# One accumulator of the first batch's first transform moves to another set of PSUM banks

## The chip, the cores and the metric

The kernel runs on one core of one Trainium2 chip. The metric is the device time of one execution in microseconds (us). Four compute engines matter: TensorE (PE, with PEld for its weight loads), VectorE (DVE), ScalarE (ACT) and GpSimd (POOL); SP only issues DMAs. TensorE writes its results into PSUM, eight banks of 2 KB per partition, from which DVE and ACT take them.

## The reference

Four batches, each of 768 positions and 8 heads of 48 channels, go through three layers: a linear recurrence (here done in chunks of 96), a token mixer that takes the real part of a 2-D Fourier transform, and two dense blocks.

```python
attn_out = _attn_ref(**attn_kwargs)              # per head: S = a*S + k v^T (a complex), y = q . Re(S)
x = attn_out.transpose(0, 2, 1, 3).reshape(B, S, H * D)   # 4 x 768 x 384
# _moe_ref
X = np.fft.fft(x, axis=1)
X = np.fft.fft(X, axis=2)
u = x + np.real(X)
un = (u - mean(u)) / np.sqrt(var(u) + 1e-06)
x = u + np.maximum(un @ w_ch1, 0.0) @ w_ch2
# _moe2_ref: a token mixer (w_tok1, w_tok2) and a second dense block (w_ch1, w_ch2), both added to x
```

## The kernel before

Each batch has a chain and a dense part. The chain is the scan and the attention chunks (`stage1`), then the Fourier mixer with its normalisation (`stage2`), then the transposes of the normalised rows (`transposed`). The dense part (`mlp`, `tok1`, `tok2`, `mlp2`) is nearly all matmuls of 128x128 weights with 384 columns (lines L1034, L1056, L1260, L1278). The dense part of one batch runs beside the chain of the next. The chain of the first batch has no dense work beside it: TensorE's long run starts when that chain ends. To keep TensorE occupied there, `warm` (L347) puts in matmuls whose results nobody reads. The weights arrive as 64-bit floats. `convert` turns each half block into a pair of fp32r blocks in six steps on ACT (L214, L219, L239), DVE (L227, L233) and POOL (L229, L240), loads it on SP (L206) and stores the result for the later batches (L244). Twelve half blocks whose loads came early are converted beside the first batch's `stage2`; most of the others follow, one by one, beside the first batch's dense part.

A planner in the compiler's tile layer puts the instructions in order before the run. Each instruction has a priority (class `Prio`: by stream, then by place in the program), and the planner places the ready one of the best priority on each engine, by its own estimate of times, and gives each new tile a free bank of its tag. On the chip each engine then works strictly in that order.

PSUM tiles come from `palloc(tag, shape)`. The tags have 8 banks in all: `s` 2, `l` 3, `p` 2, `c` 1. A call with `"s"` is spread over several tags by a counter, `turn3`, that goes up by one at each such call: while `lent` is 0, as in the whole chain of the first batch, the tags are s, s, c in turn; later it is s alone (scan of batch 1) or s and p in turn (its `stage2`), then s, s, c again. A call with `"l"` leaves the counter alone. In `stage2` of the first batch, `l` serves `warm` and the small tiles `q` of the normalisation; afterwards it serves the dense part.

In `stage2`, `folds` (L1093, L1099) and `mirrors` (L1109, and copies of single columns, L1116) prepare four kinds of rows, `ty` 0 to 3. `dft(1)` and then `dft(0)` run the first transform: for each `ty` four fp32 matmuls, which are eight instructions in the trace (L1125), into one PSUM tile, and one ACT copy of it into `Z` (L1127). With the counter as it stands, `dft(1)` gets the tags s, c, s, s and `dft(0)` gets c, s, s, c for `ty` 0 to 3; the program as built runs the four of `dft(0)` in the order 1, 2, 0, 3. Then come three rounds `i`: the second transform (`smm`, L1152, L1157), an ACT copy of its result (L1188), its difference and sum on POOL (L1189, L1190), transposes of the tokens (L1199), four additions into `u` on DVE (L1204), the statistics, a Newton step for the inverse root (L1221 to L1226) and the normalised rows (L1231 on ACT, L1233 on DVE). Round 0 reads `Z` of `ty` 0 and 1, round 1 all four, round 2 `ty` 2 and 3.

Of the kernel before, what the change touches and what calls it, by code (L numbers as in the profile page):

```python
# [54 lines left out]
def attn_fft_mixer_kernel(ctx: ExitStack, tc: tile.TileContext, aL, xL, vL, wL, qN, kN, vN, arN, aiN,  # L55
# [47 lines left out]
    def palloc(tag, shape):  # L103
        n = 1
        for s in shape[1:]:
            n *= s
        if tag == "s":
            turn3[0] += 1
            tag = ("ssc", "s", "sp")[lent[0]]
            tag = tag[turn3[0] % len(tag)]  # L110
        t = psum.tile([128, 512], F32, tag=tag, bufs=PSB[tag], name=tag)
        v = t[0:shape[0], 0:n]
        if len(shape) == 3:
            v = v.rearrange("p (a b) -> p a b", b=shape[2])
        return v
# [952 lines left out]
    def stage2(b, space):  # L1068
# [50 lines left out]
        def dft(kt):  # L1119
            for ty in range(4):  # L1120
                n0, n = 128 * kt, ZK[ty][kt]
                ps = palloc("s", [128, 2, 97])
                for r in range(2):
                    for dt in range(2):
                        te.matmul(out=ps[0:n, r, :], lhsT=fd[:, ty, r, dt, n0:n0 + n], rhs=dcos[0:112, ty % 2, dt, r, :],  # L1125
                                  start=(dt == 0), stop=(dt == 1))
                se.copy(out=Z[0:n, 2 * ty + kt, :].rearrange("p (i r) -> p r i", r=2), in_=ps[0:n])  # L1127

        for k, (o, n) in enumerate(XP[b][:-1]):
            folds(k, o, n)  # L1130
        mirrors(*NR[0])
        dft(1)
        folds(len(XP[b]) - 1, *XP[b][-1])
        x = mirrors(*NR[1])
        if b == 0:
# [4 lines left out]
            for _ in range(5):  # L1140
                tick(0)
            rests[0] = None
        dft(0)

        if b == 0 and WZ:
# [29 lines left out]
        for i in range(3):  # L1175
            ps = palloc("s", [128, 2, 193])
# [285 lines left out]
```

## Time and profile before

| | |
|---|---|
| median of 3 runs | 1025.44 us (1022.24 to 1027.12) |
| profiled execution | 1025.11 us |
| its span (first to last instruction) | 1023.2 us |
| PE busy | 951.0 us, 93% of the span |
| DVE, ACT, POOL busy | 716.9, 526.4, 452.8 us |

The busy time is summed over the whole span, and the share of the first batch's chain differs much from that of the rest. The profile is of one execution; what lies outside its span is 1.9 us.

### The profile page before, as it was taken

To read this page: it belongs to the slowest core of one execution; us is meant where nothing else is said; L and a number is where in the kernel's file an instruction comes from. 1 tells how busy PE (TensorE), PEld (TensorE's weight loads), DVE (VectorE), ACT (ScalarE), POOL (GpSimd) and SP (SyncE) were. 2 spreads that over 40 slices of the span, in tenths; PEclk is the share of its full clock that TensorE was granted. 3 is DMA by queue.
4 is the path that set the end of the run, shared out by engine and by line. 5 is a ranking of instruction groups with operands and counts; after the bars stand their busy time and mean duration, and the time that the engine had idled before them with its cause. 6 is when DMAs were issued, how large, how long until landed. Compare 5 with 4: busy or idle time off the path is not lost.

```text
span 1023.2 us, 21015 instructions
## 1 busy us (share of the span) xinstructions
PE 951.0 (93%) x7312; PEld 902.0 (88%) x7312; DVE 716.9 (70%) x1965; ACT 526.4 (51%) x1489; POOL 452.8 (44%) x655
## 2 busy tenths in 40 slices
PE   1479989999899999999999999999999999999997
PEld 0338869999898899999998999999989999999997
DVE  7988978889897778999668889855664333433332
ACT  7864568887995166887216667821342122211111
POOL 7744677765785673677147335614630002000000
PEclk9999999999999999999999999999999999999999
DMA  6625865886689435665734467553325345435422
GB/s 234 175 67 140 290 269 165 283 268 210 212 258 272 146 95 187 193 179 174 206 110 140 129 193 247 157 149 102 108 78 166 131 131 171 139 108 176 136 91 80
DMA packets 98337, 173.09 MB, mean 169 GB/s; under 512 B 10928, under 2 KB 57904, under 8 KB 97712
## 3 DMA queue, kind: packets, MB, share of 16 engines
q1 hardware_dynamic: 98224, 171.67, 53.8%
q8 instruction: 60, 0.98, 0.4%
q14 instruction: 53, 0.43, 0.1%
HBM read 132.31 MB, written 39.32 MB: 168 GB/s over the span
## 4 chain that ended last, share of the span: by engine, by line
PE 66%; DVE 6%; ACT 3%; DMA 2%; POOL 2%; issue 2%; SPq 0%; POOLq 0%; ACTq 0%; DVEq 0%
PE l L1056 25%; PE l L1034 23%; DMA cvt<-wL 2%; PE s L845 2%; PE s L721 2%; PE l L1260 1%; PE l L1278 1%; PE s L1260 1%; PE s L1278 1%; PE s L1152 1%; DVE qkt L1099 1%; PE s L900 1%; PE s L860 1%; PE c L721 1%; PE c L845 1%
## 5 line engine op out<-in xcount | busy, mean ns | idle before, releaser
L1056 PE MATMUL l<-w,h 128*128 128x384 f32 x1728 | 324.0, 339 | 1.5 <-DVE h L1047 1.0
L1034 PE MATMUL l<-th,w 128*128 128x384 f32 x1152 | 313.3, 341 | 2.8 <-DVE h L1047 2.5
L1056 PEld LDWEIGHTS l<-w,h 128*128 128x128 f32 x1728 | 298.2, 188 | 3.5 <-DVE h L1047 2.0
L1034 PEld LDWEIGHTS l<-th,w 128*128 128x128 f32 x1152 | 209.1, 188 | 5.8 <-DVE h L1047 3.9
L1038 ACT ACTIVATE h<-l 128x384 fp32r<-128x384 f32 x192 | 94.0, 490 | 215.9 <-PE l L1034 215.3
L1034 PE MATMUL l<-tl,w 128*128 128x384 f32 x576 | 194.6, 338 | 0.0
L1059 DVE TENSOR_TENSOR u<-u,l 128x384 f32<-128x384 f32 x192 | 105.5, 549 | 74.4 <-PE l L1056 73.4
L1047 DVE SCALAR_TENSOR_TENSOR h<-l,h 128x384 fp32r<-128x384 f32 x160 | 88.3, 552 | 88.9 <-ACT h L1038 88.8
L1034 PEld LDWEIGHTS l<-tl,w 128*128 128x128 f32 x576 | 108.4, 188 | 0.1
L229 POOL TENSOR_TENSOR cvt<-cvt 128x384 int32<-128x384 int32 x48 | 50.4, 1051 | 27.4 <-DVE cvt L225 16.5
L1245 POOL TENSOR_TENSOR xl<-u,xh 128x384 fp32r<-128x384 f32 x18 | 18.0, 1014 | 93.2 <-ACT xh L1244 93.0
L240 POOL TENSOR_TENSOR w<-cvt,w 128x384 fp32r<-128x384 f32 x44 | 45.0, 1027 | 13.1 <-ACT w L239 13.0
L1045 POOL TENSOR_TENSOR h<-full,h 128x384 fp32r<-128x384 f32 x32 | 32.5, 1016 | 34.3 <-ACT full L1044 32.8
L529 PE MATMUL s<-misc,y 128*112 128x128 f32 x64 | 14.5, 369 | 35.4 <-DVE y L511 27.9
L694 DVE TENSOR_TENSOR p<-p,A 128x144 f32<-128x144 f32 x144 | 44.7, 310 | 2.8 <-ACT A L671 1.0
L529 PEld LDWEIGHTS s<-misc,y 128*112 128x112 f32 x64 | 9.3, 177 | 41.6 <-POOL ss L496 20.3
L881 POOL TENSOR_TENSOR yc<-Aa,gm 48x384 f32<-48x384 f32 x18 | 20.6, 1147 | 53.3 <-DVE Aa L871 53.0
L670 POOL TENSOR_TENSOR A<-raw,tm 128x144 f32<-128x144 f32 (+1 forms) x51 | 25.9, 508 | 39.4 <-DVE yt L695 29.6
L696 DVE TENSOR_TENSOR p<-p,yt 128x96 f32<-128x96 f32 x144 | 37.7, 262 | 2.8
L651 POOL TENSOR_TENSOR tm<-tm 128x144 f32<-128x144 f32 (+1 forms) x51 | 25.3, 496 | 32.3 <-ACT tm L650 27.8
L695 DVE TENSOR_TENSOR yt<-p,A 128x96 f32<-128x96 f32 x144 | 36.2, 251 | 2.4 <-ACT A L674 0.5
L721 PE MATMUL s<-misc,y 128*112 128x128 f32 x222 | 35.5, 273 | 1.2 <-DVE y L708 0.8
(320 smaller groups left out, 2045.2 us busy)
## 6 DMA issues: line engine op xcount, KB each, us to landing
w<-wscr SPq DMA_DIRECT2D x180, 384.0 KB, 3.5
cvt<-wL SPq DMA_DIRECT2D x48, 384.0 KB, 4.8
wscr<-w SPq DMA_DIRECT2D x44, 384.0 KB, 4.1
Kn<-kn SPq DMA_DIRECT2D x56, 192.0 KB, 3.7
kn<-y SPq DMA_DIRECT2D x96, 96.0 KB, 2.7
raw<-aL SPq DMA_DIRECT2D x48, 144.0 KB, 3.8
xx<-xL SPq DMA_DIRECT2D x48, 144.0 KB, 3.6
V<-vL SPq DMA_DIRECT2D x32, 144.0 KB, 3.0
```

The costliest lines, as they stand in the source:

```text
L229: x = ge.tensor_tensor(out=a, in0=a, in1=lo, op=ALU.add)
L240: ge.tensor_tensor(out=parts[:, 1, :], in0=a.bitcast(F32), in1=r32(parts[:, 0, :]), op=ALU.subtract)
L694: ve.tensor_tensor(out=cur, in0=prev, in1=A[:, j, 0:3, :], op=ALU.mult)
L695: ve.tensor_tensor(out=y, in0=prev[:, 1::-1, :], in1=A[:, j, 3:5, :], op=ALU.mult)
L696: ve.tensor_tensor(out=cur[:, 0:2, :], in0=cur[:, 0:2, :], in1=y, op=ALU.add)
L721: te.transpose(ps[:, j, :], y[:, j, 0:112], ident)
L1034: te.matmul(out=ps, lhsT=w1[:, wi, kt * 128:kt * 128 + 128], rhs=x[g][:, kt, :], start=(n == 0), stop=(n == 8))
L1038: x = se.activation(out=hi, in_=ps, func=ACTF.Relu)
L1045: ge.tensor_tensor(out=lo, in0=full, in1=r32(hi), op=ALU.subtract)
L1047: ve.scalar_tensor_tensor(out=lo, in0=ps, scalar=0.0, in1=r32(hi), op0=ALU.max, op1=ALU.subtract)
L1056: te.matmul(out=ps, lhsT=hs[m][:, hi, tt * 128:tt * 128 + 128], rhs=w2[:, wi, :], start=(n == 0), stop=(n == 8))
L1059: ve.tensor_tensor(out=u[tt], in0=u[tt], in1=ps, op=ALU.add)
```

## The change

One call of `palloc` in `dft` takes the tag `l` where it took `s`, for the first batch, the second call (`kt` = 0) and the fourth kind (`ty` = 3). The counter `turn3` therefore stands one lower at every later call with `"s"`, in this and all later batches: where the order was s, c, s, s | c, s, s, c | s, s, c, ... it is s, c, s, s | c, s, s, l | c, s, s, ...

```diff
@@ -1119,7 +1119,7 @@
         def dft(kt):
             for ty in range(4):
                 n0, n = 128 * kt, ZK[ty][kt]
-                ps = palloc("s", [128, 2, 97])
+                ps = palloc("l" if b == 0 and not kt and ty == 3 else "s", [128, 2, 97])
                 for r in range(2):
                     for dt in range(2):
```

## Rows read from the trace of the kernel before

**Rows 1.** The page: span, then busy time of each engine.
```profile
span 1023.2 us, 21015 instructions
...
PE 951.0 (93%) x7312; PEld 902.0 (88%) x7312; DVE 716.9 (70%) x1965; ACT 526.4 (51%) x1489; POOL 452.8 (44%) x655
```
**Rows 2.** Windows by stage: stretch, length, busy us per engine, granted clock, DMA.
```profile
0.00:155.00 155.00, 103.77 (x951) 79.10 (x952) 128.92 (x399) 98.32 (x273) 97.11 (x143) 0.96 0.62 194
155.00:1023.00 868.00, 847.27 (x6362) 822.90 (x6360) 588.01 (x1567) 428.06 (x1217) 355.71 (x513) 1.00 0.53 165
...
155.00:360.00 205.00, 195.05 (x1566) 185.28 (x1564) 174.69 (x461) 152.49 (x432) 143.93 (x191) 1.00 0.71 226
```
**Rows 3.** Timeline of PE: start, duration, line, out<-in, count, idle before and releaser.
```profile
126.73 1.03 PE L1125 MATMUL s<-dcos,qkt 112*128 112x97 f32 x8
...
128.59 1.02 PE L1125 MATMUL s<-dcos,qkt 112*128 112x97 f32 x8
129.45 1.06 PE L1125 MATMUL c<-dcos,qkt 112*128 112x97 f32 x8
131.71 1.13 PE L1125 MATMUL c<-dcos,qkt 112*128 112x97 f32 x8 [1.20 <-ACT qkt L1127]
132.68 1.50 PE L1152 MATMUL s<-qkt 128*128 128x193 f32 x8
...
155.15 1.34 PE L1034 MATMUL l<-th,w 128*128 128x384 f32 x3
```
**Rows 4.** Timeline of ACT, 131 to 141 us.
```profile
131.33 0.33 ACT L1127 COPY qkt<-c 128x194 f32<-128x194 f32 x1
132.58 0.52 ACT L214 ACTIVATE p<-cvt 128x384 f32<-128x384 f32 x1 [0.93 <-DVE cvt L233]
...
133.44 0.34 ACT L1127 COPY qkt<-c 128x194 f32<-128x194 f32 x1
134.22 0.48 ACT L1188 COPY qkt<-s 128x386 f32<-128x386 f32 x1 [0.45 <-PE s L1152]
...
140.89 0.48 ACT L1188 COPY qkt<-s 128x386 f32<-128x386 f32 x1
```
**Rows 5.** Timeline of POOL, 134 to 144 us, and a window of its run.
```profile
134.80 1.02 POOL L229 TENSOR_TENSOR cvt<-cvt 128x384 int32<-128x384 int32 x1
135.77 0.54 POOL L1189 TENSOR_TENSOR qkt<-qkt 128x193 f32<-128x193 f32 x1
...
143.53 0.53 POOL L1189 TENSOR_TENSOR qkt<-qkt 128x193 f32<-128x193 f32 x1
...
129.98:145.49 15.51, 13.74 (x80) 10.85 (x80) 12.18 (x30) 8.69 (x25) 15.51 (x19) 1.00 0.72 286
```
**Rows 6.** Timeline of DVE, 136 to 149 us.
```profile
136.34 0.85 DVE L1204 TENSOR_TENSOR u<-s,qkt 128x192 f32<-128x192 f32 x2
...
143.45 2.26 DVE L1233 TENSOR_SCALAR qkt<-u,mv,rs 128x384 f32<-128x384 f32 x1
...
148.82 0.45 DVE L1233 TENSOR_SCALAR qkt<-u,mv,rs 128x384 f32<-128x384 f32 x1
```
**Rows 7.** Windows around the start of the dense part, columns as in Rows 2.
```profile
148.00:149.00 1.00, 0.30 (x3) 0.06 (x1) 1.00 (x3) 0.00 (x0) 0.10 (x1) 0.92 0.06 25
...
150.00:154.00 4.00, 3.75 (x12) 2.18 (x11) 2.58 (x8) 3.76 (x13) 1.12 (x3) 0.50 0.60 204
...
155.50:156.00 0.50, 0.50 (x3) 0.19 (x1) 0.33 (x2) 0.50 (x2) 0.00 (x0) 0.83 0.71 173
```
**Rows 8.** Timeline of SP, ACT and PE, 197 to 207 us, and SP's waits, 155 to 250.
```profile
197.72 0.42 SPq L206 DMA_DIRECT2D cvt<-wL  x1
...
204.00 0.51 ACT L214 ACTIVATE c<-cvt 128x384 f32<-128x384 f32 x1 [2.21 <-DMA cvt<-wL]
...
206.95 0.45 PE L1034 MATMUL l<-th,w 128*128 128x384 f32 x1 [1.65 <-DVE h L1047]
...
SPq L244 <- POOL cvt L240: 8.1, 2, 6.4
```

## The prediction

> **What bounds the kernel now.** I read the page first: TensorE is busy 951.0 of 1023.2 us [rows 1]. Then I cut the span at the point where the first batch's chain ends and the dense part begins, 155.15 us [rows 3]. Behind the cut TensorE is busy 847.27 of 868 us; before it, 103.77 of 155 [rows 2]. So behind 155 us TensorE itself is the bound, and what the chain of the first batch saves is worth its full size only if it brings the first matmul of the dense part (L1034 at 155.15) forward. The reader should next look at the place of the edit in the timeline of PE: three groups of `dft(0)` follow each other with only `warm` between them, then PE stands for 1.20 us until the ACT copy L1127 has ended, and only then the fourth group runs [rows 3]. Both of the last two groups have the one bank of tag `c`: the third is `ty` 0, the fourth `ty` 3. ACT copies `ty` 0 out at 131.33, for 0.33 us, and the fourth group starts at 131.71, 0.05 us behind its end [rows 3, 4]. That is the wait the edit touches.
>
> **What the change removes.** The fourth group goes to a bank of `l`. In the first batch's `stage2` the earlier holders of the three `l` banks are the matmuls of `warm`, on PE itself, whose results nobody reads, so no other engine has to release that bank. The wait of 1.20 us goes. The number of instructions is the same: eight matmuls and one copy, before and after.
>
> **What is late next on PE.** The fourth group can follow the third, which ends at 129.45 + 1.06 = 130.51 us [rows 3]. With its 1.13 us it ends near 131.64. Behind it on PE stands round 0 of the second transform (L1152), which reads `Z` of `ty` 0, that is, the copy that ends at 131.33 + 0.33 = 131.66 [rows 4]. So L1152 starts at about 131.71 where it started at 132.68 [rows 3]: PE wins 0.97 us, not 1.20.
>
> **What is late next on ACT.** L1152 of round 0 takes 1.50 us [rows 3], so it would end at 133.21 instead of 134.18, and its ACT copy L1188, at 134.22 now [rows 4], could start at 133.25. In ACT's order a conversion step (L214, 132.58) and the copy of `ty` 3 (133.44 to 133.78) stand ahead of it [rows 4]. If that order stays, L1188 starts at 133.78, 0.44 earlier; if the planner moves the copy of `ty` 3 up, by up to 0.97. I carry 0.44 to 0.97.
>
> **Where it ends.** L1188 hands over to POOL. Its copy was complete at 134.22 + 0.48 = 134.70, but POOL took up L1189 only at 135.77, since a conversion step (L229, from 134.80, 1.02 us) stood before it [rows 4, 5]. In round 2 it is plainer: the input was there at 140.89 + 0.48 = 141.37 and POOL came to it at 143.53 [rows 4, 5]. POOL is busy for 15.51 of the 15.51 us from 129.98 to 145.49 [rows 5]. It is the bound of this stretch: it converts weights, and the rounds stand in its queue. The additions into `u` (L1204, 136.34) start behind POOL's pair [rows 5, 6]. So an input that comes 0.44 to 0.97 us earlier waits that much longer in front of POOL, as long as POOL's order stays. Even where the planner puts the pair one conversion step earlier (1.02 us [rows 5]), a second barrier follows on DVE. L1233 took 2.26 us at 143.45 and 0.45 us in the next round at 148.82 [rows 6]; the long one ends at 145.71, 0.22 us behind the end of POOL's run. Being ready earlier gives it nothing as long as it is held to the end of that run, and the run's length is set by the number of steps in it, which the edit doesn't change.
>
> The Trainium skill, "SBUF — State Buffer", section "Who interferes with whom", says that a DVE instruction such as `tensor_scalar` in a two-port mode and a GpSimd instruction exclude each other for one whole instruction, whichever came first. By that rule L1233 would have had its turn after the POOL step that was running, not after three more; this trace disagrees, with 2.26 us and an end behind the run. Were the rule to hold after the change, the result is the first rival's time.
>
> **The sum.** The removed wait is -1.20 us on PE, of which 0.97 reaches L1152, 0.44 to 0.97 reaches L1188, and 0 gets past POOL's run. Cost of the edit at nothing: covered by POOL's 15.51 us; with that cover gone, -0.97. Other terms: the granted clock is 0.92 in 148 to 149 us, 0.50 (1.2 GHz) in 150 to 154 and back on the way up at 0.83 in 155.5 to 156 [rows 7], after TensorE has had pauses between the transposes. With PE done earlier and the rest in place, a pause before 149 grows by up to 0.97 us, and the level could fall that much earlier; 0.97 us at half speed does 0.49 us less of full-speed work. No row shows which, so the term lies between -0.49 and +0.49 (the rise may come earlier too), and I take 0, since the pauses that precede the fall end on DVE, which doesn't move. The shift of the counter costs nothing by itself: three banks are used in rotation before and after; round `i` of the second transform takes `c` instead of a bank of `s`, and in both cases the bank that it takes has been emptied by a copy that the round before, or `ty` 0's `Z`, demands anyway. Sum: 0, with bounds -1.20 and +0.49. The profiled execution took 1025.11 us (its span and 1.9 us around it), 0.33 under the median of the three runs. My forecast is 1025.11 + 0 = 1025.1 us.
>
> **The rivals.** First, the gain goes through: the planner sees the input ready earlier, places the pair L1189, L1190 a step earlier in all rounds, and L1233 finds a gap in POOL's run. Then the dense part starts 0.97 to 1.20 us earlier, and since PE is 98% busy behind it, the end does too: 1023.9 to 1024.1 us. For it speaks that POOL's order isn't fixed by hand; against it, the 2.26 us of L1233.
>
> Second, slower: a load of a weight slips. The planner's order beyond 155 us rests on its estimates, and an earlier time here, with the counter shifted, can change the order of many instructions. The place where that hurts is the conversion beside the first dense part. The load L206 at 197.72 is the example: ACT stood 2.21 us for it before L214 at 204.00, the eviction of the dense part stood behind L214 in ACT's and DVE's order, and PE waited 1.65 us at 206.95 [rows 8]. There is no slack at that place, so any further delay of a load passes to PE whole. SP works in order, and its longest wait for POOL in front of a store L244 is 6.4 us [rows 8]; a load placed behind such a store is 6.4 us later. Price: +6.4, 1031.5 us. It decides as soon as one load falls behind one such store.
>
> Third, faster by more: the same order changes for the better. PE is idle 205 - 195.05 = 9.95 us between 155 and 360 us [rows 2], by conversions, scans and evictions. If half of it goes, with the 0.97, that is -5.9: 1019.2 us.
>
> Fourth, the edit doesn't do what it says: the planner lets the fourth group wait for something else (an `l` bank that isn't free by its estimate, or a place behind L1152's first group). Then PE's 1.20 us stands under another name, at 1025.1 us.
>
> **How the numbers follow.** Absorbed at POOL: 0.46. Gain goes through: 0.25. Slower: 0.12. Faster by more: 0.12. Wait not removed: 0.05. A measurement of this kernel can tell about 0.5%, 5.1 us, from no change; so faster by more than that 0.12, within it 0.46 + 0.25 + 0.05 = 0.76, slower 0.12. The likeliest cases alone span 1023.9 to 1025.6. The range reaches towards the second and third rivals, over the 1.7 to 3.2 us by which the lowest and highest run lie from the median, and stops short of their full price: 1019.5 to 1030.5.
>
> **What would show it.** After the change the idle 1.20 us before the fourth group should be gone and L1125 of `ty` 3 should write `l`; L1152 should start about 1 us earlier; POOL's run should still end within a few tenths of 145.5 us; L1233 should again be long and end just behind that run; L1034 should start at 154.9 to 155.3. The forecast is wrong if POOL's run ends more than 0.5 us earlier or L1233 takes 0.45 us in round 0 (then the first rival), or if PE's idle time from the start of the dense part to 360 us changes from 9.95 us by more than 2 us (then the second or third).

## The result: slower by 0.8%, above the range

The changed kernel takes 1031.9 us (median of nine runs, 1029.0 to 1039.0) where the kernel before takes 1024.1 in the same series; the ratio is 1.0082, with a 95% interval of 1.0064 to 1.0100. (Ratios are taken over all runs of a series; they need not be the quotient of two medians.) A second series of the same kernel gives 1031.17 us and 1.0067 [1.0041, 1.0092]. The forecast was 1025.1 with no change, and its range ended at 1030.5.

The profiled execution of the changed kernel took 1029.0 us, the shortest of the nine, so its trace shows only part of the loss. The page of the changed kernel, its span and the busy time of each engine, to be read beside [rows 1]:

```profile
span 1027.1 us, 21019 instructions
...
PE 952.6 (93%) x7312; PEld 902.2 (88%) x7312; DVE 719.0 (70%) x1965; ACT 528.3 (51%) x1489; POOL 452.4 (44%) x655
```

Windows by stage of the changed kernel (columns as in [rows 2]):

```profile
0.00:155.00 155.00, 103.40 (x953) 77.17 (x953) 128.66 (x398) 97.63 (x273) 96.34 (x142) 0.97 0.63 194
155.00:1027.00 872.00, 849.16 (x6361) 825.00 (x6359) 590.33 (x1568) 430.65 (x1218) 356.03 (x514) 0.99 0.53 164
155.00:360.00 205.00, 195.54 (x1566) 185.97 (x1565) 176.96 (x462) 152.82 (x435) 147.46 (x196) 0.99 0.72 229
```

Against [rows 2] the first 155 us are as before. The stretch behind them is 4.0 us longer (872 for 868), and PE's 4.0 us divide into two kinds: idle time 22.84 for 20.73 us, +2.1, and busy time 849.16 for 847.27, +1.9, with the same matmuls. So part of the loss is pauses and part is slower matmuls. The idle time from 155 to 360 us is 9.46 for 9.95: the loss isn't in the place that the prediction's second rival named, but later.

**The place of the edit.** PE's timeline in the changed kernel, the answer to [rows 3]:

```profile
129.80 0.61 PE L1125 MATMUL c<-dcos,qkt 112*128 112x97 f32 x4
130.25 0.83 PE L1125 MATMUL l<-dcos,qkt 112*128 112x97 f32 x6
130.92 0.61 PE L1125 MATMUL c<-dcos,qkt 112*128 112x97 f32 x4
131.36 0.39 PE L1125 MATMUL l<-dcos,qkt 112*128 112x97 f32 x2
131.59 0.63 PE L1199 MATMUL s<-misc,xT 112*128 112x112 f32 x4
132.06 0.64 PE L1199 MATMUL s<-misc,qkt 112*128 112x112 f32 x4
132.53 1.52 PE L1152 MATMUL c<-qkt 128*128 128x193 f32 x8
...
154.81 1.09 PE L1034 MATMUL l<-th,w 128*128 128x384 f32 x3
```

The fourth group writes `l`, and the idle 1.20 us in front of it is gone. The planner interleaves it with the third, so the bank `c` is complete at 131.53 and not at 130.51, and two groups of transposes (L1199) go ahead of the second transform. L1152 starts at 132.53 where it started at 132.68. The third group itself starts 0.35 us later in this trace (129.80 for 129.45), so counted from it L1152 comes 0.50 us earlier, 2.73 us behind it for 3.23. POOL's run and the long instruction on DVE, the answers to [rows 5, 6]:

```profile
130.71:146.23 15.52, 13.79 (x77) 10.44 (x76) 12.18 (x30) 8.53 (x25) 15.52 (x19) 1.00 0.74 294
```
```profile
144.18 2.26 DVE L1233 TENSOR_SCALAR qkt<-u,mv,rs 128x384 f32<-128x384 f32 x1
```

POOL's run has the same length, 15.52 us for 15.51, and L1233 takes the same 2.26 us and ends 0.21 us behind the end of the run (0.22 before). The dense part starts at 154.81 for 155.15.

Single times of this stretch carry little, since it differs from trace to trace. Nine of the kernels below run the first batch as the kernel before does; in their traces the dense part starts between 153.41 and 157.36 us, and the first L1233 takes 0.48 us in six, 1.48 in one and 2.25 or 2.26 in two. In all seven traces with the move it takes 2.26 to 2.28. Counted from the start of the third group, the dense part follows after 25.1 to 29.0 us without the move (25.70 in the kernel before) and after 25.0 to 26.2 with it.

**Where the time goes.** Each kernel runs 3744 dense matmuls (L1034, L1056, L1260, L1278). I numbered them in the order of PE's timeline and read off when numbers 720, 1296, 1728 and 2448 start. That gives three stretches that can be laid side by side: A (from about 302 us) holds the attention and `stage2` of the second batch, B those of the third, C the scan, attention, `stage2` and transposes of the last batch. In the kernel before they take 165.17, 135.38 and 185.82 us. Behind number 2448 the trace is the same to 0.5 us in every kernel but the second experiment's.

| kernel | A | B | C | ratio [95%] |
|---|---|---|---|---|
| changed | +0.99 | +1.68 | +3.38 * | 1.0082 [1.0064, 1.0100] |
| changed, second series | +2.35 | +1.45 | +1.80 | 1.0067 [1.0041, 1.0092] |

(us against the kernel before; * the granted clock falls to 0.5 behind a pause in C). The three sum to +6.1 us, of which C has 3.4. Idle time of PE is a steadier measure than these lengths, which take in the clock: in C it is 2.43 us before, 4.41 in the changed kernel and 4.40 in the second series. In the trace shown, number 720 starts 1.8 us earlier (301.07 for 302.87), and so number 2448 4.3 us later (793.50 for 789.24). The start of number 720 varies without a pattern, from 299.6 to 303.3 us, in all kernels below but the second experiment's. PE's timeline in C, first of the kernel before and then of the changed one:

```profile
759.32 1.81 PE L1056 MATMUL l<-w,h 128*128 128x384 f32 x9
761.60 0.55 PE L1012 MATMUL s<-misc,qkt 128*128 128x128 f32 x3 [0.47 <-ACT qkt L1231]
762.98 0.55 PE L1012 MATMUL c<-misc,qkt 128*128 128x128 f32 x3 [0.84 <-ACT qkt L1231]
763.28 1.99 PE L1260 MATMUL s<-xh,w 128*128 128x384 f32 x10
```
```profile
760.69 0.94 PE L1056 MATMUL l<-w,h 128*128 128x384 f32 x4
761.47 0.49 PE L1012 MATMUL c<-misc,qkt 128*128 128x128 f32 x3
765.25 2.92 PE L1260 MATMUL c<-xh,w 128*128 128x384 f32 x10 [3.29 <-DVE tl L1018]
...
768.92 0.77 PE L1012 MATMUL s<-misc,qkt 128*128 128x128 f32 x3
```

Before, PE loses 0.47 + 0.84 = 1.31 us here; after, it stands for 3.29 us in one piece, +1.98. Then the same ten matmuls L1260 take 2.92 us where they took 1.99, because the clock is granted at its lower level, 1.2 GHz. The window of the changed kernel (granted clock in the third column from the right):

```profile
766.00:769.50 3.50, 3.50 (x15) 3.40 (x13) 0.00 (x0) 0.43 (x1) 0.64 (x1) 0.51 0.02 5
```

3.5 us at 0.51 do 1.7 us less work; 1.98 + 1.7 = 3.7 is near the +3.38 of the table. DVE shows why PE stands. The last Newton step of the batch (L1225), first before, then after:

```profile
758.34 0.15 DVE L1225 TENSOR_TENSOR rs<-rs 128x2 f32<-128x2 f32 x1
...
761.68 0.54 DVE L1059 TENSOR_TENSOR u<-u,l 128x384 f32<-128x384 f32 x1
```
```profile
761.67 0.55 DVE L1059 TENSOR_TENSOR u<-u,l 128x384 f32<-128x384 f32 x1 [0.83 <-PE l L1056]
762.14 0.68 DVE L1225 TENSOR_TENSOR rs<-rs 128x2 f32<-128x2 f32 x1
762.85 0.92 DVE L1226 SCALAR_TENSOR_TENSOR rs<-rs 128x2 f32<-128x2 f32 x1
763.69 0.55 DVE L1018 TENSOR_TENSOR tl<-s,th 128x384 fp32r<-128x384 f32 x1
764.16 0.56 DVE L1230 SCALAR_TENSOR_TENSOR rs<-mv,rs 128x2 f32<-128x2 f32 x1
764.65 0.55 DVE L1018 TENSOR_TENSOR tl<-c,th 128x384 fp32r<-128x384 f32 x1
```

Before, the step starts 3.3 us ahead of the last addition of the dense block (L1059). After, it stands behind that addition, which itself waits for PE's last L1056. So when the normalisation of the last batch is worked off, PE is through with L1056, and the next dense matmul in its order, L1260, waits for its bank.

The smaller parts have the same form. In A, PE waits for `mirrors` (L1109) in the second batch. One such pause, of 1.47 us before and 1.49 after, is in both kernels; the second is longer, and DVE's timeline shows why, before and after:

```profile
357.74 1.67 DVE L1109 TENSOR_TENSOR qkt<-qkt 112x190 f32<-112x190 f32 x6
359.34 0.54 DVE L1059 TENSOR_TENSOR u<-u,l 128x384 f32<-128x384 f32 x1
```
```profile
355.13 1.14 DVE L1109 TENSOR_TENSOR qkt<-qkt 112x190 f32<-112x190 f32 x4
356.19 0.54 DVE L1059 TENSOR_TENSOR u<-u,l 128x384 f32<-128x384 f32 x1
356.66 3.28 DVE L1109 TENSOR_TENSOR qkt<-qkt 112x190 f32<-112x190 f32 x2
```

Six of them ran in 1.67 us; now an addition stands between the fourth and the fifth, and the last two take 3.28 us, 2.72 of them the fifth. PE, before and after:

```profile
360.46 1.56 PE L1125 MATMUL p<-dcos,qkt 112*65 112x97 f32 x8 [0.32 <-POOL qkt L1109]
```
```profile
359.53 0.88 PE L1125 MATMUL p<-dcos,qkt 112*65 112x97 f32 x4 [1.77 <-DVE qkt L1109]
```

In B, PE reaches the attention of the third batch (L860), which needs a load (`Kn`). Before, nine dense matmuls stand directly in front of it and it doesn't wait; after, six end at 491.90 and PE stands for 1.39 us. Before and after:

```profile
493.20 1.82 PE L1278 MATMUL l<-R,w 128*128 128x384 f32 x9
```
```profile
490.69 1.21 PE L1278 MATMUL l<-R,w 128*128 128x384 f32 x6
493.30 0.23 PE L860 MATMUL s<-V,Kn 96*64 96x48 f32 x1 [1.39 <-DMA Kn<-kn]
```

None of these places is near the edit, and none of their instructions was edited. What reaches them is the counter `turn3`. Theory one: the loss is the price of the counter's shift in the later batches. Theory two: it is the price of the move itself or of what the first batch does differently, carried on. Theory three, for C: two tiles meet in the one bank of `c`.

### The profile page after: what moved, and what is told of

It is laid out like the page before. It is cut to its first block, busy times and chain, and to the rows that moved or that the text cites. A ratio compares the mean times of both kernels' runs of the same rounds, so it can differ in the third digit from the quotient of the medians.

```text
span 1027.1 us, 21019 instructions
## 1 busy us (share of the span) xinstructions
PE 952.6 (93%) x7312; PEld 902.2 (88%) x7312; DVE 719.0 (70%) x1965; ACT 528.3 (51%) x1489; POOL 452.4 (44%) x655
## 4 chain that ended last, share of the span: by engine, by line
PE 64%; DVE 7%; POOL 3%; DMA 2%; issue 2%; ACT 2%; SPq 0%; POOLq 0%; ACTq 0%; DVEq 0%
PE l L1056 25%; PE l L1034 23%; DMA cvt<-wL 2%; PE s L721 2%; PE s L845 1%; PE l L1260 1%; POOL w L240 1%; POOL cvt L229 1%; PE s L900 1%; DVE qkt L1109 1%; PE c L845 1%; PE s L1278 1%; DVE qkt L1099 1%; PE c L1260 1%; PE s L1125 1%
## 5 line engine op out<-in xcount | busy, mean ns | idle before, releaser
L1056 PE MATMUL l<-w,h 128*128 128x384 f32 x1728 | 324.6, 339 | 0.9 <-DVE h L1047 0.7
L1034 PE MATMUL l<-th,w 128*128 128x384 f32 x1152 | 315.3, 341 | 2.2 <-DVE h L1047 1.8
L1056 PEld LDWEIGHTS l<-w,h 128*128 128x128 f32 x1728 | 297.5, 188 | 3.2 <-DVE h L1047 1.6
L1034 PEld LDWEIGHTS l<-th,w 128*128 128x128 f32 x1152 | 209.1, 188 | 4.1 <-DVE h L1047 2.8
L1034 PE MATMUL l<-tl,w 128*128 128x384 f32 x576 | 194.1, 337 | 0.0
L1059 DVE TENSOR_TENSOR u<-u,l 128x384 f32<-128x384 f32 x192 | 105.7, 550 | 75.9 <-PE l L1056 74.8
L1034 PEld LDWEIGHTS l<-tl,w 128*128 128x128 f32 x576 | 108.6, 188 | 0.2
L240 POOL TENSOR_TENSOR w<-cvt,w 128x384 fp32r<-128x384 f32 x44 | 45.2, 1032 | 14.5 <-ACT w L239 14.2
```

The lines of the kernel that those rows point to most:

```text
L240: ge.tensor_tensor(out=parts[:, 1, :], in0=a.bitcast(F32), in1=r32(parts[:, 0, :]), op=ALU.subtract)
L1034: te.matmul(out=ps, lhsT=w1[:, wi, kt * 128:kt * 128 + 128], rhs=x[g][:, kt, :], start=(n == 0), stop=(n == 8))
L1056: te.matmul(out=ps, lhsT=hs[m][:, hi, tt * 128:tt * 128 + 128], rhs=w2[:, wi, :], start=(n == 0), stop=(n == 8))
L1059: ve.tensor_tensor(out=u[tt], in0=u[tt], in1=ps, op=ALU.add)
```

## The experiments

All times are medians, all ratios are against the kernel before in the same series. Its medians in the four series that follow were 1024.79 us (the first two kernels below, the shift in the last batch, and the last batch put right), 1023.96 (the second series of the changed kernel, the shift in the first, second and third batch), 1023.6 (third and last together, the bank and the order in C, the third phase) and 1025.11 (scan and `stage2` apart).

**The move without the shift.** The changed kernel, with the counter advanced as before:

```diff
-                ps = palloc("l" if b == 0 and not kt and ty == 3 else "s", [128, 2, 97])
+                ps = palloc("l" if b == 0 and not kt and ty == 3 else "s", [128, 2, 97]); turn3[0] += b == 0 and not kt and ty == 3
```

> The group moves to a bank of l, but the counter is advanced as in the kernel before, so every later tile has the tag that it had. Counter theory (the loss of 7.8 us comes from the shifted counter, through the pause of 3.29 us before L1260 at 765 us and longer stretches at half clock; the move itself wins 0.3 to 1.8 us): 1022.3 to 1023.8 us, and no pause over 1 us before L1260. Move theory (a tile of dft in an l bank upsets the order of the dense part): 1030 to 1033 us. Theory of the forecast (absorbed at POOL): 1024.1 us.

1024.79 us beside 1024.79 of the kernel before: 0.9999 [0.9987, 1.0011]. Compared place by place along the traces, by source line alone, 26 of PE's 7312 instructions and 3 of ACT's are others than in the kernel before, all ahead of 141 us; in the changed kernel it is 1757 on PE and 588 of DVE's 1965, up to 785 us. The trace:

```profile
131.11 0.39 PE L1125 MATMUL l<-dcos,qkt 112*128 112x97 f32 x2
132.18 1.58 PE L1152 MATMUL s<-qkt 128*128 128x193 f32 x8 [0.69 <-ACT qkt L1127]
...
155.61 0.92 PE L1034 MATMUL l<-th,w 128*128 128x384 f32 x2
```

L1152 starts 0.50 us earlier than before (0.59 counted from the third group), and L1034 not earlier at all. L1233 again takes 2.26 us. The gain of 0.3 to 1.8 us that the counter theory gave the move doesn't show. So the move alone is worth nothing that can be measured, and it costs nothing.

**The shift without the move.** The kernel before, with the counter put one back at the same call:

```diff
-                ps = palloc("s", [128, 2, 97])
+                ps = palloc("s", [128, 2, 97]); turn3[0] -= b == 0 and not kt and ty == 3
```

> The group stays in the bank that it had; only the counter is set back by one behind it, as the change does to all later tiles. Counter theory: slower by 6 to 10 us, 1030 to 1034 us, with a pause of some 3 us before L1260 near 765 us. Move theory: 1024 us, as before.

1042.18 us, 1.0170 [1.0142, 1.0197], more than was expected. It is no clean half of the change: here three tiles in a row have `c` (`ty` 0, `ty` 3 and round 0), where in the changed kernel the second of them has `l`. The dense part starts only at 159.41 us, and the whole order behind differs. It says that the rotation matters; its size belongs to another case.

**The shift in one batch at a time.** These let the first batch alone and set the counter at the points where the chains of the later batches begin. For the second batch (kernel before, the shift put in and taken out again):

```diff
-        lent[0] = int(not b)
+        lent[0] = int(not b); turn3[0] += (-1, 1)[b]
```

> The kernel before, with the counter set back by one only in the chain of batch 1, where the tags are s and p in turn, and put right again behind it. If the s/p parity of batch 1 carries the loss (in the changed kernel's trace its stage2 has pauses of 1.5 and 1.8 us before L1125 and 6.8 us at half clock instead of 3.4): 1028 to 1031 us, with the long L1109 on DVE (some 3.3 us for two) near 357 us. If it carries nothing: 1024.5 us.

For the third:

```diff
-        lent[0] = int(not b)
+        lent[0] = int(not b); turn3[0] -= b
...
-    u1, norm = on(CHAIN, chain, B - 1)
+    turn3[0] += 1; u1, norm = on(CHAIN, chain, B - 1)
```

> The kernel before, with the counter set back by one only in the chain of batch 2. If batch 2 carries its share (+2.3 us between 382 and 763 us in the changed kernel's trace): 1026 to 1028 us, with a pause of over 1 us before L860 near 494 us. If it carries nothing: 1024.5 us.

For the last:

```diff
-    u1, norm = on(CHAIN, chain, B - 1)
+    turn3[0] -= 1; u1, norm = on(CHAIN, chain, B - 1)
```

> The kernel before, with the counter set back by one only from the chain of the last batch on. If the tags at the tail are the cause: slower by 4 to 6 us, 1028 to 1030 us, with the pause of 3 us before L1260. If they are not: 1024 us.

For the third and the last together:

```diff
-        lent[0] = int(not b)
+        lent[0] = int(not b); turn3[0] -= b
```

> The kernel before, with the counter one lower from the third batch on (batches 2 and 3), and batches 0 and 1 as before. If the parts add up, the shift of the third batch (1.0036) and that of the last (1.0023) together give 1.0059, in bounds of 1.0045 to 1.0075, 1030.0 us where the kernel before has 1024; the pauses at 493 us (1.4 us) and ahead of L1260 near 765 us (3.3 us) are both there. If the loss in the changed kernel comes from batches 0 and 1 instead, or from the move, it is 1.002 to 1.004.

And the changed kernel with the counter put right from the second batch on, so that only the first batch differs from the kernel before:

```diff
-        lent[0] = int(not b)
+        lent[0] = int(not b); turn3[0] += not b
```

> The changed kernel with the counter put right again before batch 1: the group is in an l bank and the rest of the first batch has the shifted tags, all later batches those of the kernel before. If the loss needs later batches' tags: 1024 to 1025 us, as e1_move_only. If the shifted tags in the first batch carry it: 1029 to 1032 us.

| shifted in | us | A | B | C | ratio [95%] |
|---|---|---|---|---|---|
| first batch alone, with the move | 1023.89 | -0.86 | 0.00 | -0.03 | 1.0008 [0.9989, 1.0026] |
| second | 1025.44 | +2.73 | -0.08 | -0.01 | 1.0011 [0.9996, 1.0025] |
| third | 1028.02 | -0.94 | +1.18 | +2.90 * | 1.0036 [1.0021, 1.0052] |
| last | 1026.86 | -0.55 | -0.22 | +1.78 | 1.0023 [1.0007, 1.0039] |
| third and last | 1029.17 | -1.00 | +3.12 | +3.37 * | 1.0053 [1.0038, 1.0067] |

Each shift brings back the loss in its own stretch and in no earlier one, that of the third batch in the stretch behind it as well. The pair third and last gives 0.53%, and 0.36 + 0.23 = 0.59 lies within its interval. PE's idle time in C doesn't add up so: it grows by 0.99 us with the third batch, 1.99 with the last and 1.98 with both. The last batch alone has its pause of 3.29 us ahead of L1260, as expected, but costs some 2 us and not 4 to 6; in its trace the clock doesn't fall behind the pause. With the second batch's 0.11 the parts sum to 0.70%, beside 0.82 and 0.67 for the whole change. Theory two is out: with the move and the shifted first batch alone nothing is lost that can be measured. The second batch's part is the weakest: one trace shows +2.73 us in A, the same 3.28 us for two L1109 in it, but the runs show 0.11% with an interval that holds zero, 1025.44 us between the two expectations. A also varies between traces where nothing in it was changed (from -1.00 to +2.17 us).

**The last batch put right.** The changed kernel, with the counter advanced by one ahead of the last chain alone (`turn3[0] += 1; u1, norm = on(CHAIN, chain, B - 1)`).

> The changed kernel, with the counter put right again from the chain of the last batch on (the tags of all tiles behind that place are those of the kernel before). If the loss sits in the tags of the last batch's chain and of the mixed dense part: 1024.5 to 1026 us, no pause before L1260. If it comes from the tags of batches 1 and 2 or from an order that was upset at the start: 1029 to 1033 us.

1032.63 us, 1.0076 [1.0052, 1.0101]: nothing came back that can be told from the changed kernel. The trace has +3.33, +1.50 and +1.36 us in A, B and C. C still has a pause of 2.00 us ahead of L1012, as with the third batch's shift alone, and 0.99 us more idle time than before (1.98 in the changed kernel). So the ratios of the parts add, within their intervals, where each is put into the kernel before, but one part taken out again gives nothing back that the runs can tell.

**Is it the bank, in C?** In the changed kernel the late accumulator L1260 has the bank `c` behind the fourth transposed tile, and waits for DVE to empty it. Two kernels take that apart. In one the pair of accumulators has `s`, `s`:

```diff
-        pss = [palloc("s" if late else "l", [128, 384]) for _ in range(2)]
+        turn3[0] += b == B - 2; pss = [palloc("s" if late else "l", [128, 384]) for _ in range(2)]; turn3[0] -= b == B - 2
```

> The changed kernel, but the two late accumulators of the third batch's token mixer (L1260) both take s, as they do in the kernel before; all other tags stay as in the changed kernel (the transposed tiles of the last batch c, s, s, c, s, s). Theory bank: the pause of 3.29 us ahead of L1260 at 765 us comes from the first accumulator having the one bank of c behind the fourth transposed tile. Without it the stretch from the 2160th to the 2448th dense matmul falls from 82.6 us (81.0 in the second profile of the changed kernel) to 78.5 to 79.5 (78.5 before), and the ratio to the kernel before from 1.0082 to 1.0050 to 1.0065. Theory late chain: the last batch's chain is 3.5 us later against the dense work in the changed kernel, so the pause moves to another instruction (a transpose L1012 or L1034) at about its size, and the ratio stays at 1.007 to 1.0085.

In the other the tags stay, but L1260 is ordered behind all six transposes:

```diff
-    LAST = [None]
+    LAST = [None, None]
...
-                tp = te.transpose(px[:, dt, :], src[:, dt * 128:dt * 128 + 128], ident)
+                tp = te.transpose(px[:, dt, :], src[:, dt * 128:dt * 128 + 128], ident); LAST[-1] = tp
...
-                        te.matmul(out=pss[m2], lhsT=w, rhs=x[kt], start=(kt == 0 and not low and w is wh),
-                                  stop=(kt == 5 and low == 1))
+                        mm = te.matmul(out=pss[m2], lhsT=w, rhs=x[kt], start=(kt == 0 and not low and w is wh),
+                                  stop=(kt == 5 and low == 1)); b == B - 2 and after(mm, LAST[-1])
```

> The changed kernel, with all its tags, but in the planner's order the late accumulators of the third batch's token mixer (L1260) come only behind the last batch's six transposes (L1012), as they do in the kernel before. Theory order: PE stands for 3.29 us at 765 because two transposes that could run are placed behind L1260; with them in front PE has work and the pause is 1.5 us or less, the ratio 1.005 to 1.0065. Theory bank: the first accumulator still waits for the one bank of c, which the fourth transposed tile holds until DVE has taken it, and that step stands behind the late chain in DVE's order: the pause stays at 2.5 to 3.5 us in sum and the ratio at 1.007 to 1.0085.

The first measures 1030.93 us, 1.0068 [1.0051, 1.0085], between its two expectations, and the second 1030.0 us, 1.0057 [1.0043, 1.0071]. The traces decide. PE's timeline of the first, and then of the second:

```profile
762.90 0.49 PE L1012 MATMUL c<-misc,qkt 128*128 128x128 f32 x3
766.95 0.55 PE L1012 MATMUL s<-misc,qkt 128*128 128x128 f32 x3 [3.56 <-ACT qkt L1231]
```
```profile
768.13 0.49 PE L1012 MATMUL c<-misc,qkt 128*128 128x128 f32 x3
772.17 1.86 PE L1012 MATMUL s<-misc,qkt 128*128 128x128 f32 x6 [3.56 <-ACT qkt L1231]
```

In both the wait for the bank is gone, and the same pause, 3.56 us, stands ahead of the fifth transpose, which waits for the normalised rows (L1231). C is +4.27 and +4.65 us. So theory three falls as the cause of the loss, and the order that was tried doesn't help either: the chain of the last batch is late, and in both kernels another instruction waits for it. Neither kernel gives L1260 a bank that no other tile of that stretch uses. In the changed kernel its first inputs (`xh`) are written from 760.25 us on, before `c` is empty at 765.20, so whether a free bank would shorten the pause is not shown. The ratio of the second lies within what was expected of the order, but its trace has no shorter pause, so I don't count it for that. (That trace is of the slowest of its seven executions, 1037.12 us, and has +5.05 us in B.)

**What makes the chain late?** The scan of a batch and its `stage2` both draw from the rotation. Four kernels shift one of them alone, all from the kernel before. The last batch, scan alone:

```diff
-        return stage2(b, stage1(b))
+        x = stage1(b); turn3[0] += b == B - 1; return stage2(b, x)
...
-    u1, norm = on(CHAIN, chain, B - 1)
+    turn3[0] -= 1; u1, norm = on(CHAIN, chain, B - 1)
```

> The kernel before, with the counter one lower in the scan of the last batch alone; from its stage2 on all tags are those of the kernel before. Theory scan: the last batch's chain is late since the order of its scan steps is another one; its folds (L1099) come 1.5 us later against the dense work, and the stretch from the 2160th to the 2448th dense matmul is 80 to 81.5 us (78.5 before, 81.0 with the tags of the whole last batch shifted); ratio 1.001 to 1.003. Theory late tags: the loss comes from the tags of stage2 and of the transposed tiles; the scan's shift alone leaves the stretch at 78 to 79, ratio 0.999 to 1.001.

The last batch, from `stage2` on:

```diff
-        return stage2(b, stage1(b))
+        x = stage1(b); turn3[0] -= b == B - 1; return stage2(b, x)
```

> The kernel before, with the counter one lower from the last batch's stage2 on, its scan as before. Theory scan: without the late scan the chain ends as before, and the stretch from the 2160th to the 2448th dense matmul stays at 78 to 79 us, the ratio at 0.999 to 1.001. Theory late tags: the transposed tiles and the late accumulators meet in c, so L1260 waits about 3 us and the stretch is 80 to 81.5 us, ratio 1.001 to 1.003.

The third batch, scan alone:

```diff
-        return stage2(b, stage1(b))
+        x = stage1(b); turn3[0] += b == 2; return stage2(b, x)
...
-        lent[0] = int(not b)
+        lent[0] = int(not b); turn3[0] -= b
```

> The kernel before, with the counter one lower in the scan of the third batch alone. Theory scan: the third batch's loss lies here too; the stretch from the 1296th to the 1728th dense matmul is 136.5 to 138.5 us (135.4 before, 136.6 with the tags of the whole batch shifted), with a pause of 1 us or more near 493 us ahead of L860, and the ratio is 1.002 to 1.004. Theory late tags: 135 to 136 us, no pause near 493 us, ratio 0.999 to 1.0015.

The third batch, from `stage2` to its transposes:

```diff
-        return stage2(b, stage1(b))
+        x = stage1(b); turn3[0] -= b == 2; return stage2(b, x)
...
-    u1, norm = on(CHAIN, chain, B - 1)
+    turn3[0] += 1; u1, norm = on(CHAIN, chain, B - 1)
```

> The kernel before, with the counter one lower from the third batch's stage2 to its transposed tiles, its scan and the last batch as before. Theory scan: 135 to 136 us from the 1296th to the 1728th dense matmul, ratio 0.999 to 1.0015. Theory late tags: the 1.1 us more in stage2's part (60.4 us from the 1440th to the 1584th dense matmul instead of 58.2) is here, the stretch is 136.5 to 138.5 us, ratio 1.002 to 1.004.

| shifted | us | B | C | ratio [95%] |
|---|---|---|---|---|
| last batch, scan | 1028.23 | -0.19 | +4.63 * | 1.0036 [1.0016, 1.0056] |
| last batch, behind the scan | 1023.66 | +0.04 | -0.03 | 0.9992 [0.9976, 1.0008] |
| third batch, scan | 1030.70 | +2.84 | +4.06 * | 1.0064 [1.0038, 1.0090] |
| third batch, behind the scan | 1029.37 | -0.64 | +4.27 * | 1.0041 [1.0023, 1.0059] |

In the last batch it is the scan. PE's timeline in C with the scan shifted, and then with all behind it shifted:

```profile
758.14 0.49 PE L1012 MATMUL s<-misc,qkt 128*128 128x128 f32 x3
762.18 0.90 PE L1012 MATMUL s<-misc,qkt 128*128 128x128 f32 x3 [3.56 <-ACT qkt L1231]
```
```profile
759.67 0.55 PE L1012 MATMUL s<-misc,qkt 128*128 128x128 f32 x3 [0.47 <-ACT qkt L1231]
761.05 0.55 PE L1012 MATMUL s<-misc,qkt 128*128 128x128 f32 x3 [0.84 <-ACT qkt L1231]
761.36 1.99 PE L1260 MATMUL c<-xh,w 128*128 128x384 f32 x10
```

The second has L1260 in `c`, as in the changed kernel, and loses the same 0.47 + 0.84 us as the kernel before, so L1260 in `c` costs nothing where the chain is on time. The same kernel parts the renaming from the order: 226 of PE's instructions write another tag than before, PE's order is that of the kernel before in all 7312 places, and nothing is lost. With the scan shifted the folds L1099 start 1.55 us later against the dense work than in the kernel before (112.68 for 111.13 us behind matmul 1728), and the last Newton step 2.87 us later (157.80 for 154.93). From number 2160 to 2448 it is 83.9 us and not the 80 to 81.5 that were expected, since the clock falls at the pause. The lateness is the same wherever the pause is: in the nine traces that have a pause of some 3.3 us or more in C and in the two with 2.0 us, the last Newton step starts 157.1 to 157.9 us behind matmul 1728; in the kernel before and all others but the second experiment's it is 154.9.

In the third batch neither theory holds. The expectations looked for the loss in B; with the scan shifted B has 2.84 us of it, and with the rest shifted none, but in both the larger part is in C. Either part alone measures as much as both together or more (0.64 and 0.41% beside 0.36, with intervals that overlap), and both lengthen C, in which nothing of the third batch's chain stands. Both put off the chain of the last batch against the dense work: PE's pause near 765 us is 3.84 us in either. The larger part of their +4.06 and +4.27 us is matmuls at the lower clock: PE's idle time in C grows by 1.43 and 1.44 us. So here it isn't one tile or one bank: each of the three shifts by one leaves the last chain with less dense work beside its end, though that chain has its old tags. The shift the other way, below, doesn't.

**The third phase.** The kernel before, with the counter one higher, not lower, from the third batch on (`turn3[0] += b` at the same place).

> The kernel before, with the counter one higher from the third batch on, the third of the three phases that the rotation s, s, c can have there; neither the kernel before nor the changed one has it. Theory fitted: the kernel before has the one phase to which the third and the last batch are fitted, and each other phase makes PE wait somewhere: 1.003 to 1.010. Theory of any order: the phases differ only by the order that the planner happens to find, so a third phase is as likely faster as slower: 0.995 to 1.005. The late accumulators of the token mixer have s and then c here, so the first of them has no need to wait for a transposed tile of the last batch in c, and the pause ahead of L1260 should be under 1.5 us.

1027.16 us, 1.0027 [1.0012, 1.0043]; B +3.35 us, C 0.00, and the last transposes wait 0.46 and 0.84 us as before, within the 1.5 us that were expected. The ratio lies below the 1.003 to 1.010 of the theory of a fitted phase and within the 0.995 to 1.005 of the other, but its interval leaves out 1. Of the two stretches that were changed, the third phase loses in B only. Of the rotation's three phases from the third batch on, that of the kernel before is the best and the changed kernel's the worst, by these ratios (1.0053 for the shift from the third batch on). With three phases that is no proof that the others must lose.

## Why the prediction was wrong, point by point

- **The wait removed.** Right: the 1.20 us is gone and `ty` 3 writes `l`.
- **0.97 us reach L1152.** Too large for these traces: counted from the third group it is 0.50 us in the changed kernel and 0.59 in the move alone (0.15 and 0.50 on the clock of the trace). The working let the fourth group follow the third; the planner interleaved them, so `c` was complete 1.73 us behind the third group's start and not 1.06.
- **0 gets past POOL's run.** The size is right: the move alone measures 0.9999. The reason is borne out by the profiles before and after, and not beyond them. In these two the run lasts 15.52 for 15.51 us, and L1233 takes 2.26 again and ends 0.21 us behind the run. But in six other traces with the old first batch L1233 takes 0.48 us beside a busy POOL, and the dense part follows the third group after 25.1 to 29.0 us, beside 25.70. So it isn't shown that this barrier fixes the start, and what does stays open. By the Trainium skill's "SBUF — State Buffer", section "Who interferes with whom", L1233, if it works in a two-port mode, which no row tells, would have had its turn after one POOL step; the trace of the changed kernel disagrees a second time. The run itself moved, though: it begins 0.73 and ends 0.74 us later, at 146.23, and not within a few tenths.
- **The clock term.** The lower level at 150 to 154 us that [rows 7] show is not there after; that window is granted 1.00 (0.77 in the move alone). The term was put at 0 since DVE wouldn't move; L1233 starts 0.73 us later. In the first 155 us this was worth little, 154.81 for 155.15 in all.
- **"The shift of the counter costs nothing by itself: three banks are used in rotation before and after".** This step failed. It looked at the first batch's rounds, where it holds (1.0008), and took them for all. The shift renames the banks of the later tiles of the chains, the planner then finds another order (1757 of PE's 7312 places), and the order of the kernel before was better by 0.36% in the third batch and 0.23% in the last. The renaming itself is indeed free: where it left the order alone, behind the last batch's scan, the ratio is 0.9992. The term stood at 0 and measures 7 to 8 us in the runs.
- **The second rival** had the side and, by chance, the size (+6.4 for +7.8), and said that another order of many instructions was the way. Its place and mechanism were wrong: SP's longest wait for POOL in front of such a store is 5.5 us for 6.4, and PE's idle time from 155 to 360 us fell by 0.5 us. So no sign of being wrong that the prediction named came: the one for this rival looked at the stretch to 360 us alone, and the loss is behind it. Its chance, 0.12, was too small because it was priced as one slip at one place, while the counter acts on three batches.
- **The range.** It ended at 1030.5 for a cause that can't be bounded by one row. What could have been read from the trace before is where an order matters: PE's waits at 761.60 and 762.98 show that the last chain ends with hardly any dense work beside it. There 2.9 us of delay gave PE 2.0 to 2.7 us more idle time, and where the clock fell behind it, some 1.7 us of full-speed work or more were lost besides.

What stays open: why the planner's other orders bring the last chain later, which would need its own estimates of time; and how much of the median's 7.8 us is clock. The two profiled executions of the changed kernel are 3.9 and 2.9 us above that of the kernel before (1029.0 and 1028.0 for 1025.1), less than the medians. The mean granted clock was 0.987 over the nine runs and 0.989 over the second series' six, beside 0.992 over the 29 runs of the kernel before in that series. Mean span times mean clock is 1017.5 and 1017.1 us for the changed kernel and 1014.1 for the kernel before, so by that estimate some 3 us are order and the rest, 3 to 5 us, is clock. No run separates the two.

## What to carry to other kernels

A counter that hands out banks in rotation couples every later tile to the one that is edited: when a call leaves the rotation, advance the counter as before, and measure the move and the shift apart. Where a planner orders the work, price a renaming not by the banks' number but by the places where the order is tight: find in the trace the stretches where a chain ends with no dense work left beside it, and ask what a few microseconds of delay cost there. When a pause moves to another instruction at the same size, as from L1260 to L1012 here, look for what both wait for.

## What the runs showed of the hardware

DVE and POOL can each keep the other out for longer than one instruction. In the kernel before, six L1109 on DVE take 0.34 us each, one behind the other from 357.74 us, and the L1109 that POOL has begun takes 2.78 us; its next one takes 0.59. In the changed kernel the addition stands between the fourth and the fifth on DVE; the fifth takes 2.72 us, to 0.21 us behind the end of three POOL instructions in a row (L1109, L240, L240), and the sixth 0.64. POOL is busy throughout in both (1.67 of 1.67 and 3.28 of 3.28 us), so a busy POOL alone doesn't make DVE slow. The Trainium skill, "SBUF — State Buffer", section "Who interferes with whom", says that a DVE instruction with two SBUF inputs contends with a GpSimd instruction that reads SBUF; the trace agrees, with 2.72 us for 0.34. L1233, with one such input, took 2.26 us in the kernel before, in the changed one and in the move alone, but 0.48 us in six traces, beside a busy POOL too.

The granted clock can fall behind a pause of PE, also late in the kernel: behind the 3.29 us in C it was 0.51 in the changed kernel, and the ten matmuls behind cost 0.93 us more. In the second series' trace the same kernel had the same pause and no fall there (C +1.80 for +3.38). So one order has more than one time: the changed kernel's runs range from 1029.0 to 1039.0 us in the first series and from 1027.5 to 1033.1 in the second, those of the kernel before from 1022.2 to 1027.1 and from 1021.7 to 1030.0.
